# x kept in DRAM as two float16 halves scaled by batch, and an expert's rows turned by transposing DMAs instead of by TensorE

## The chip, the cores and the metric

One NeuronCore of a Trainium2 chip runs the whole program; the other seven are idle. The metric is the time of one execution in microseconds (us) as the device reports it. The engines are TensorE (PE, with its weight loads shown apart as PEld), VectorE (DVE), ScalarE (ACT), GpSimd (POOL) and SyncE (SP), which here only issues DMAs. Each engine works through its own instructions in the order in which they are written, and so does each queue of DMA issues.

## The reference, cut to what matters

```python
# attention: batch 4, heads 8, seq 768, head_dim 64, 16 clusters
q_assign = argmax(q_n @ c_n.T); k_assign = argmax(k_n @ c_n.T)
mask = q_assign[..., :, None] == k_assign[..., None, :]
attn = softmax(where(mask, scale * q @ k.T, -1e9)) @ v
x = attn.transpose(0, 2, 1, 3).reshape(3072, 512)
# mixture of experts: 8 experts, two for each row
noisy = x @ w_gate + log1p(exp(x @ w_noise)) * noise
top2 and their softmax weights wt, for each row
for e in range(8):
    out[rows of e] += wt * (relu(x[rows of e] @ w1[e]) @ w2[e])     # w1: 512x1024, w2: 1024x512
```

All inputs and the output are float32.

## The kernel before

**The attention** runs over 16 pairs of heads, four pairs to a batch. It is written as 192 steps, twelve for each pair. A step makes two score tiles of 128x384 (`scores`, L515), takes their exponential on ACT (L516), and four steps later multiplies an earlier step's exponentials by v (`values`, L544 to L550). Around this core a table `AT` and the function `at(step, f)` put every other piece of work at a third of a step: splitting q and k into halves (`a_split`, L382 to L392), the row maxima (`b_max`, L484 and L487), the cluster mask (`a_mask`, `b_mask`, L448 to L456), and loads. The order of each engine is this written order. All score tiles, transposes and small sums pass through one ring of six PSUM buffers (`ps()`, tile name `ring`): TensorE can't begin the seventh tile after one that ACT or VectorE has not yet read.

When the last pair of batch b is done, its x rows lie in `xt[b]` (128 partitions, six rows of 512 float32 each). `store_x(b)` writes them to the DRAM tensor `xs` in one DMA of 1.5 MB (L591), and `g_logits`, `g_logits2`, `g_turn`, `g_gate` and `g_list` work out the gate and write each row's number and weight into a table of the experts' rows. For batches 0 to 2 this lies among the steps of the next batch, from step 48b + 52 on. For batch 3 it lies in `experts`, beside the first expert's first layer.

**The experts** take at most 832 rows each, in seven tiles (six of 128, one of 64). For a tile, `gather_x` (POOL, L1125) fetches 128 rows of `xs` by an indirect DMA into `xg` (four buffers). `turn_x` (L1136) turns it: four transposes on TensorE into a ring buffer, and then `scaled_halves` writes a high and a low float16 half, times `sx`, into `xT` (ACT L1035, VectorE L1036). `sx` is one power of two for the whole of x: `x_max` takes the maximum of |v| over all batches (an upper bound of |x|), and `x_scale` (L1046 to L1057) makes `px` and its reciprocal `sx` from it. `layer1` (L1146) multiplies each of eight column blocks of w1 by `xT` in three products of halves, ACT and VectorE write relu halves into `hT`, and `layer2` (L1183; L1174 and L1177 for the short tile) makes 128 rows of output, which VectorE weighs (L1192) and POOL scatters (L1196).

There is one `xT`. The next expert's turns stand between this expert's second-layer tiles (`tail`), after its first layer has read `xT`. Weights go through seven staging buffers (`stg`, L1104 for w1, L1113 for w2), are reduced to a maximum and split into halves on ACT and VectorE.

The first expert is special: its first four tiles (`TA`) hold rows of batches 0 to 2 alone, so its first layer over these runs while batch 3 is gated; three further tiles are gathered after batch 3's list is known, and its first layer over them runs after the first four second-layer tiles.

## Time and profile before

| | us |
|---|---|
| median of 3 runs | 1087.87 (1086.75 to 1088.76) |
| the profiled execution | 1087.8 |
| its span, first to last instruction | 1086.0 |
| outside the span | 1.8 |
| TensorE busy | 1024.3 (94%) |
| VectorE busy | 702.7 (65%) |
| POOL busy | 550.4 (51%) |
| ACT busy | 533.7 (49%) |
| TensorE's granted clock, mean | 0.985 of full speed |

A busy time counts every instruction from start to end; matmuls overlap, so a busy TensorE is not one at its peak. "Idle before" is the time in which an engine had nothing running before an instruction, and the releaser is the event that ended it. Idle time counts only where it lies on the engine that sets the end.

### The profile page before, as it was taken

How to read it: one execution, taken by the hardware profiler on the slowest of the kernel's cores; microseconds unless marked ns; L12 is line 12 of the kernel's file. 1: busy time of each engine (PE TensorE's matmuls, PEld its weight loads, DVE VectorE, ACT ScalarE, POOL GpSimd, SP SyncE). 2: the span in 40 equal slices, each digit the busy share in tenths (PEclk: the TensorE clock that was granted, in tenths of full speed). 3: DMA queues.
4: the chain of work that ended last, by engine and by line, in shares of the span. 5: the costliest groups of instructions: out<-in, count | busy, mean ns of one | idle time of the engine just before them, and what ended most of it. 6: DMA issues, size and time to landing. Idle time of an engine off the chain costs nothing.

```text
span 1086.0 us, 22549 instructions
## 1 busy us (share of the span) xinstructions
PE 1024.3 (94%) x8733; PEld 705.0 (65%) x8733; DVE 702.7 (65%) x1484; ACT 533.7 (49%) x1090; POOL 550.4 (51%) x598
## 2 busy tenths in 40 slices
PE   5789999999999999979999999999999999999994
PEld 4678898889888988865555555555455555554542
DVE  5787776977688768998375656645655565556511
ACT  3467767766776766665144425334254152432510
POOL 9167675779677977831344233442352333513211
PEclk9799999999999999999999999999999999999997
DMA  7776767576757655252235235342352344422200
GB/s 199 170 186 145 177 157 201 143 170 156 206 141 177 155 158 116 81 176 93 98 114 174 92 110 174 117 136 100 125 183 72 100 160 137 136 82 77 59 33 34
DMA packets 87058, 144.48 MB, mean 133 GB/s; under 512 B 13689, under 2 KB 65273, under 8 KB 86434
## 3 DMA queue, kind: packets, MB, share of 16 engines
q1 hardware_dynamic: 73650, 106.61, 36.5%
q0 software_dynamic: 13296, 36.38, 10.3%
q8 instruction: 70, 1.15, 0.4%
q14 instruction: 42, 0.34, 0.1%
HBM read 78.21 MB, written 26.51 MB: 96 GB/s over the span
## 4 chain that ended last, share of the span: by engine, by line
PE 72%; DVE 10%; issue 8%; POOL 4%; DMA 3%; ACT 2%; SPq 0%; POOLq 0%; DVEq 0%; ACTq 0%
PE ring L1146 21%; PE ring L1183 20%; PE ring L515 9%; PE ring L484 5%; PE av L544 2%; PE ring L1136 2%; PE av L550 2%; PE av L546 2%; DMA A<-mk 2%; DVE aux L487 2%; PE ring L403 1%; DVE mm L487 1%; PE ring L382 1%; PE ring L418 1%; DVE pl L527 1%
## 5 line engine op out<-in xcount | busy, mean ns | idle before, releaser
L527 POOL TENSOR_TENSOR pl<-pe 128x768 f16<-128x768 f32 x173 | 251.7, 1469 | 80.7 <-ACT pe L516 78.7
L1146 PE MATMUL ring<-xT,w1t 128*128 128x416 f16 (+2 forms) x1536 | 274.9, 340 | 2.3 <-DVE xT L1036 2.3
L1183 PE MATMUL ring<-w2t,hT 128*128 128x512 f16 x1152 | 255.3, 379 | 0.0
L516 ACT ACTIVATE pe<-ring,l 128x384 f32<-128x384 f32 x384 | 201.6, 578 | 64.9 <-PE ring L515 59.9
L1146 PEld LDWEIGHTS <-w1t 128*128 128x128 f16 x1536 | 149.9, 98 | 121.6 <-issue 5.1
L1183 PEld LDWEIGHTS <-hT 128*128 128x128 f16 x1152 | 112.7, 98 | 127.1
L1196 POOL DMA_INDIRECT out<-yo,idx x52 | 62.8, 1208 | 210.1 <-DVE yo L1192 107.9
L487 DVE TENSOR_REDUCE aux<-ring 128x1 f32<-128x384 f32 x192 | 108.0, 562 | 73.0 <-PE ring L484 68.5
L1029 ACT ACTIVATE hr<-ring 128x416 f32<-128x416 f32 (+2 forms) x128 | 66.5, 520 | 161.7 <-PE ring L1146 161.4
L515 PE MATMUL ring<-A 128*128 128x384 f32 x384 | 141.5, 368 | 0.9 <-ACT pe L516 0.7
L1032 DVE TENSOR_TENSOR hT<-hr,hT 128x416 f16<-128x416 f32 (+3 forms) x128 | 71.5, 559 | 100.8 <-ACT hT L1031 100.7
L515 PE MATMUL ring<-B 128*128 128x384 f32 x384 | 129.9, 338 | 1.6 <-DMA B<-nt 1.6
L1125 POOL DMA_INDIRECT xg<-xs,idx x52 | 60.7, 1167 | 117.3 <-PE ring L1136 101.4
L484 PE MATMUL ring<-A 128*128 128x384 f32 x384 | 108.3, 357 | 12.0 <-DMA A<-mk 6.6
L1192 DVE SCALAR_TENSOR_TENSOR yo<-ring,we,xt 128x512 f32<-128x512 f32 (+1 forms) x49 | 36.7, 749 | 115.2 <-PE ring L1183 102.3
L487 DVE TENSOR_REDUCE mm<-ring 128x1 f32<-128x384 f32 x192 | 105.1, 548 | 0.0
L1035 ACT ACTIVATE xT<-ring,sx 128x512 f16<-128x512 f32 (+1 forms) x56 | 36.0, 659 | 139.2 <-PE ring L1136 139.2
L544 PE MATMUL av<-vv,pe 128*128 128x65 f16 x1152 | 97.1, 195 | 2.7 <-DVE xt L558 2.6
L546 PE MATMUL av<-vv,pe 128*128 128x64 f16 x1152 | 96.2, 192 | 0.0
L544 PEld LDWEIGHTS <-pe 128*128 128x128 bf16 x1152 | 79.5, 99 | 18.0 <-issue 11.5
L484 PEld LDWEIGHTS ring<-A 128*128 128x128 f32 x384 | 69.7, 191 | 23.5 <-ACT pe L516 9.6
L546 PEld LDWEIGHTS <-pe 128*128 128x128 bf16 x1152 | 77.8, 98 | 0.3
(208 smaller groups left out, 1530.5 us busy)
## 6 DMA issues: line engine op xcount, KB each, us to landing
stg<-in_moe_w SPq DMA_DIRECT2D x64, 512.0 KB
A<-hl SPq DMA_DIRECT2D x30, 384.0 KB
B<-hl SPq DMA_DIRECT2D x30, 384.0 KB
vt<-in_v SPq DMA_DIRECT2D x8, 768.0 KB
out<-zt SPq DMA_DIRECT2D x12, 512.0 KB
xs<-xt SPq DMA_DIRECT2D x4, 1536.0 KB
A<-hl SPq DMA_DIRECT2D x60, 96.0 KB
B<-hl SPq DMA_DIRECT2D x30, 192.0 KB
```

Of the source, the lines that this page charges most:

```text
L484: nc.tensor.matmul(t, A[:, 0, s, j * 128:j * 128 + 128], A[:, 1, s, n * 384:n * 384 + 384], start=True, stop=True)
L487: nc.vector.tensor_reduce(o, t, axis=X, op=OP.max, negate=True)
L515: nc.tensor.matmul(t, M[:, 1 - qi, s, ks], M[:, qi, s, ns], start=not qi, stop=bool(qi))
L516: nc.scalar.activation(pe[:, n], t, AF.Exp, bias=self.l64[:, 0:1], scale=self.scale)
L527: (nc.vector if last else nc.gpsimd).tensor_tensor(lo, pe, hi, op=OP.subtract)
L544: nc.tensor.matmul(av[:, j, :], ph[:, js], vv[:, hh, kj, 64:129], start=(kc == 0 and j == 0), stop=False, skip_group_check=True)
L546: nc.tensor.matmul(av[:, j, :64], ph[:, js], vv[:, hh, kj, 0:64], start=False, stop=False, skip_group_check=True)
L1029: nc.scalar.activation(r[:, :n], p, AF.Relu, scale=2.0 ** -HT)
L1032: nc.vector.tensor_tensor(h1, r[:, a:b], h0, op=OP.subtract)
L1146: nc.tensor.matmul(p, self.w1t[:, wi, c, f * 128:f * 128 + 128], self.xT[:, xi, c, n0:n1], start=(i == 0), stop=(i == 3 * ND - 1))
L1183: nc.tensor.matmul(p, self.hT[:, hi, f, t * 128:t * 128 + 128], self.w2t[:, wi, f], start=(i == 0), stop=(i == 3 * NF - 1))
L1196: i = nc.gpsimd.indirect_dma_start(out=self.out, out_offset=bass.IndirectOffsetOnAxis(ap=en[:r], axis=0), in_=yo[:r], in_offset=None, boun ...
```

## The change

x is scaled and split into float16 halves once, when a batch is stored, and `xs` holds both halves of a row side by side (1024 float16, the same 2 KB). `store_x` is cut into three pieces of two rows per partition: ACT makes the high half, VectorE the low one, SP stores the 512 KB piece. The piece's buffer `xh` is one tile of a pool in which a name has one buffer unless it asks for more: `pre` for batches 0 to 2, `mo` for batch 3. A gathered tile then needs nothing but turning, and `turn_x` becomes one `dma_start_transpose` on SP's queue, from `xg` (128 x 1024 float16) to all eight 128-column blocks of `xT`. The halves must be made before the last batch's maximum is known, so the scale is now taken for each batch alone (`px`, `sx` have four columns), and the gate's weight carries `px` of its batch. Places in the written order move: the pieces of a batch stand at steps z + 1.333, 2.667 and 4.0 (z = 48b + 52), batch 3's after `split_w2(0, i)`; the first four turns stand ahead of the list load; in `tail` three turns stand ahead of the first second-layer tile and one ahead of each further one.

```diff
-        self.px, self.sx = (consts.tile([128, 1], F32, name=n) for n in ("px", "sx"))
+        self.px, self.sx = (consts.tile([128, self.B], F32, name=n) for n in ("px", "sx"))
...
-                at(z + T["store"], self.store_x, b)
+                for c in range(3):
+                    at(z + 1.333 + 1.333 * c, self.store_x, b, c)
...
-            at(z - 45 + 2 * i, self.x_scale, i)
+            for b in range(B):
+                at((48 * b + 3 if b else 20) + 2 * i, self.x_scale, b, i)
             at(z - 6 + i, self.w1_scale, 0, i)
-        at(z - 46, self.x_max)
+        for b in range(B):
+            at(48 * b + 2 if b else 19, self.x_max, b)
...
-        self.xs = self.dram.tile([N, DM], F32, name="xs")
+        self.xs = self.dram.tile([N, 2 * DM], F16, name="xs")
...
-    def store_x(self, b):
-        W = self.NJ * self.DM
-        self.nc.sync.dma_start(rap(self.xs, b * 128 * W, [[W, 128], [1, W]]),
-                               self.xt[b].rearrange("p j c -> p (j c)"))
+    def store_x(self, b, c):
+        n = self.NJ // 3
+        W, V = 2 * self.NJ * self.DM, 2 * n * self.DM
+        pool = self.pre if b + 1 < self.B else self.mo
+        h = pool.tile([128, n, 2, self.DM], F16, name="xh")
+        x, s = self.xt[b][:, n * c:n * c + n], self.sx[:, b:b + 1]
+        self.nc.scalar.activation(h[:, :, 0], x, AF.Copy, scale=s)
+        self.nc.vector.scalar_tensor_tensor(h[:, :, 1], x, s, h[:, :, 0], op0=OP.mult, op1=OP.subtract)
+        self.nc.sync.dma_start(rap(self.xs, b * 128 * W + V * c, [[W, 128], [1, V]]), h.rearrange("p j i c -> p (j i c)"))
...
-        do(lambda: nc.scalar.activation(rf()[:, :, 0, 1], pm(1), AF.Copy))
+        do(lambda: nc.scalar.activation(rf()[:, :, 0, 1], pm(1), AF.Copy, scale=self.px[:, b:b + 1]))
...
-            v.tensor_tensor(rf()[:, :, 1, 1], pm(1), m(1), op=OP.mult)
+            v.scalar_tensor_tensor(rf()[:, :, 1, 1], pm(1), self.px[:, b:b + 1], m(1), op0=OP.mult, op1=OP.mult)
...
-        self.store_x(b)
+        late = AT["late"]
+        for t in range(TA):
+            self.turn_x(0, t)
         self.load_list(1)
-        late = AT["late"]
-        for t in range(TA - late):
-            self.turn_x(0, t)
...
-            if j == NJ - 1:
-                for t in range(TA - late, TA):
-                    self.turn_x(0, t)
...
             self.split_w2(0, i)
+            if i < 3:
+                self.store_x(b, i)
...
-                while done < T and done * (T - t0) < (t - t0 + 1) * T:
+                while done < T and done < (t + 3 if e else 4 * (t - t0 + 1)):
                     self.turn_x(n, done)
...
-            self.nc.vector.tensor_tensor(self.c1, self.pw1, self.px, op=OP.mult)
+            self.nc.vector.tensor_copy(self.c1, self.pw1)
...
-        xg = self.mw.tile([128, self.DM], F32, name="xg", bufs=4)
+        xg = self.mw.tile([128, 2 * self.DM], F16, name="xg", bufs=4)
...
-        p = self.ps().rearrange("p (c n) -> p c n", c=ND)
-        for c in range(ND):
-            nc.tensor.transpose(p[:, c, :r], xg[:r, c * 128:c * 128 + 128], self.ident[:r, :r])
-        self.scaled_halves(self.xT[:, :, :, t * 128:t * 128 + r], p[:, :, :r], self.sx)
+        nc.sync.dma_start_transpose(self.xT.rearrange("p i c n -> p (i c) n")[:, :, t * 128:t * 128 + r], xg[:r])
```

`x_max` and `x_scale` take the batch as an argument and work on its columns. The same edits stand in `extra`, the loop for an expert with more than 832 rows.

## Rows read from the trace of the kernel before

**Rows 1.** The page: busy us (share of the span) and instructions of each engine; the chain that ended last, by engine.
```profile
PE 1024.3 (94%) x8733; PEld 705.0 (65%) x8733; DVE 702.7 (65%) x1484; ACT 533.7 (49%) x1090; POOL 550.4 (51%) x598
PE 72%; DVE 10%; issue 8%; POOL 4%; DMA 3%; ACT 2%; SPq 0%; POOLq 0%; DVEq 0%; ACTq 0%
```
**Rows 2.** Busy time by stage: the stretch around batch 0's store, and one expert. After the stretch and its length come busy us (instructions) of PE, PEld, DVE, ACT and POOL, TensorE's granted clock, the DMA engines' busy share and GB/s.
```profile
160.00:190.00 30.00, 29.63 (x382) 25.41 (x380) 18.92 (x47) 21.51 (x48) 15.46 (x14) 1.00 0.75 202
...
716.80:788.50 71.70, 71.70 (x388) 37.60 (x387) 41.02 (x67) 27.22 (x55) 26.52 (x34) 1.00 0.38 121
```
**Rows 3.** TensorE in order of time through the tail of expert 1: its first turn and second-layer tile, its last turn and the short tile (start, us, instruction, count). Then all turns of the program by their line (duration ns min/median/max, first and last start).
```profile
607.00 0.60 PE L1136 MATMUL ring<-ident,xg 128*128 128x128 f32 x4
607.44 5.34 PE L1183 MATMUL ring<-w2t,hT 128*128 128x512 f16 x24
...
641.47 0.46 PE L1136 MATMUL ring<-ident,xg 64*128 64x64 f32 x4
641.86 1.90 PE L1174 MATMUL ring<-w2t,hE 128*128 128x512 f16 x8
...
L1136 PE MATMUL ring<-ident,xg x224: 221/273/330, 482.1 to 1000.5; 128*128 128x128 f32 x96, 64*128 64x64 f32 x16
```
**Rows 4.** TensorE through the tail of the first expert (expert 0), and its granted clock just after (length, PE busy, clock, DMA share, GB/s).
```profile
552.25 1.47 PE L1136 MATMUL ring<-ident,xg 128*128 128x128 f32 x12
553.56 5.34 PE L1183 MATMUL ring<-w2t,hT 128*128 128x512 f16 x24
558.74 1.04 PE L1136 MATMUL ring<-ident,xg 128*128 128x128 f32 x8
559.62 5.34 PE L1183 MATMUL ring<-w2t,hT 128*128 128x512 f16 x24
564.79 0.99 PE L1136 MATMUL ring<-ident,xg 128*128 128x128 f32 x8
565.72 1.90 PE L1174 MATMUL ring<-w2t,hE 128*128 128x512 f16 x8
...
571.57 5.53 PE L1146 MATMUL ring<-xT,w1t 128*128 128x416 f16 x21 [2.33 <-DVE xT L1036]
...
572.00:574.00 2.00, 2.00 (x8) 0.50 0.55 219
```
**Rows 5.** What a DMA takes from issue to use: the landing times of the 56 gathers of 256 KB; and a 4 KB load on SP, issued at 465.90, with the POOL instruction that waits for it.
```profile
DMA to landing us min/median/max: 3.2/4.0/5.8
...
465.90 0.33 SPq L792 DMA_DIRECT2D lst<-tbl  x1
...
468.44 1.47 POOL L1125 DMA_INDIRECT xg<-xs,lst  x1 [3.56 <-DMA lst<-tbl]
```
**Rows 6.** The DMA engines while batch 2's store of 1.5 MB moves with nothing ahead of it (stretch, length, granted clock, busy share, GB/s).
```profile
400.00:401.00 1.00, 1.00 0.93 393
```
**Rows 7.** SP's issues around batch 0's store (the second of two 768 KB loads for batch 1, then the store), and the DMA engines just then (columns as in rows 6).
```profile
167.12 1.20 SPq L324 DMA_DIRECT2D qk<-in_k  x1
...
172.82 0.53 SPq L591 DMA_DIRECT2D xs<-xt  x1
...
172.00:173.00 1.00, 1.00 1.04 384
174.00:175.00 1.00, 1.00 1.15 120
```
**Rows 8.** ACT (two lines), VectorE and TensorE (two lines) in order of time in the same stretch.
```profile
168.70 0.60 ACT L600 ACTIVATE gxT<-ring 128x512 f32<-128x512 f32 x1 [2.11 <-PE ring L598]
...
171.74 0.28 ACT L609 ACTIVATE lg<-ring 128x128 f32<-128x128 f32 x1
...
167.63 0.56 DVE L439 TENSOR_TENSOR oh<-ring,km 128x384 bf16<-128x384 f32 x1
...
171.25 0.42 PE L608 MATMUL ring<-gxT,wgn 128*32 128x128 f32 x8
...
173.16 0.49 PE L382 MATMUL ring<-ident,qk 128*128 128x128 f32 x3
```
**Rows 9.** ACT in batch 2's stretch, at the place that answers to 171.74 of rows 8.
```profile
395.23 0.28 ACT L609 ACTIVATE lg<-ring 128x128 f32<-128x128 f32 x1
```
**Rows 10.** The end of the first expert's first layer over its four early tiles: two splits of w2 on ACT, one on VectorE, and the start of the second layer.
```profile
507.26 1.15 ACT L1035 ACTIVATE w2t<-stg,sw 128x1024 f16<-128x1024 f32 x1
...
517.62 1.15 ACT L1035 ACTIVATE w2t<-stg,sw 128x1024 f16<-128x1024 f32 x1
...
508.79 1.27 DVE L1036 SCALAR_TENSOR_TENSOR w2t<-stg,sw,w2t 128x1024 f16<-128x1024 f32 x1
...
516.45 15.70 PE L1183 MATMUL ring<-w2t,hT 128*128 128x512 f16 x72
```
**Rows 11.** TensorE where the experts begin, and at the turns of the three late tiles.
```profile
482.14 1.50 PE L1136 MATMUL ring<-ident,xg 128*128 128x128 f32 x12
...
491.44 2.82 PE L1146 MATMUL ring<-xT,w1t 128*128 128x512 f16 x12
...
531.99 1.42 PE L1136 MATMUL ring<-ident,xg 128*128 128x128 f32 x12
533.34 5.35 PE L1183 MATMUL ring<-w2t,hT 128*128 128x512 f16 x24
```
**Rows 12.** The one TensorE transpose of a scale (here that of w1), with what it waited for.
```profile
468.27 0.27 PE L1046 MATMUL ring<-ident,wm 128*4 128x128 f32 x1 [0.81 <-DVE wm L1068]
```

More of the change, by code (lines that the diff above doesn't have):

```diff
@@ L988, in extra @@
                                       .rearrange("p e t c -> p (e t c)"))
-                    xg = self.mw.tile([128, DM], F32, name="xg", bufs=4)
+                    xg = self.mw.tile([128, 2 * DM], F16, name="xg", bufs=4)
                     nc.gpsimd.indirect_dma_start(out=xg, out_offset=None, in_=self.xs,
@@ L996, in extra @@
                                                  bounds_check=self.N - 1, oob_is_err=False)
-                    p = self.ps().rearrange("p (c n) -> p c n", c=ND)
-                    for c in range(ND):
-                        nc.tensor.transpose(p[:, c, :], xg[:, c * 128:c * 128 + 128], self.ident)
-                    self.scaled_halves(self.xT[:, :, :, 0:128], p, self.sx)
+                    nc.sync.dma_start_transpose(self.xT.rearrange("p i c n -> p (i c) n")[:, :, 0:128], xg)
                     for f in range(NF):
@@ L1036, in scaled_halves, with x_max @@
         self.nc.vector.scalar_tensor_tensor(dst[:, 1], st, s, dst[:, 0], op0=OP.mult, op1=OP.subtract)
-    def x_max(self):
+    def x_max(self, b):
         self.xm = self.wk.tile([128, 1], F32, name="xm", bufs=1)
-        self.nc.vector.reduce_max(self.xm, self.vm.rearrange("p g h -> p (g h)"), axis=X)
+        self.nc.vector.reduce_max(self.xm, self.vm[:, 2 * b:2 * b + 2].rearrange("p g h -> p (g h)"), axis=X)
     def scale_a(self, m):
@@ L1057, in scale_b, with x_scale @@
         nc.vector.reciprocal(s, p)
-    def x_scale(self, i):
+    def x_scale(self, b, i):
         if i == 0:
@@ L1062, in x_scale @@
         else:
-            self.scale_b(self.xg_, self.fx, self.px, self.sx)
+            self.scale_b(self.xg_, self.fx, self.px[:, b:b + 1], self.sx[:, b:b + 1])
     def max_w1(self, e, c):
@@ L1133, in turn_x @@
         xg = self.xg.pop((e, t))
-        p = self.ps().rearrange("p (c n) -> p c n", c=ND)
-        for c in range(ND):
-            nc.tensor.transpose(p[:, c, :r], xg[:r, c * 128:c * 128 + 128], self.ident[:r, :r])
-        self.scaled_halves(self.xT[:, :, :, t * 128:t * 128 + r], p[:, :, :r], self.sx)
+        nc.sync.dma_start_transpose(self.xT.rearrange("p i c n -> p (i c) n")[:, :, t * 128:t * 128 + r], xg[:r])
     def layer1(self, e, f, parts):
```

## The prediction

> **What bounds the kernel now.** I read the page first, then the busy times by stage, then TensorE in order of time. The page gives TensorE 94% of the span, and the chain that ended last runs 72% through it [rows 1]. By stage it is closer still: around batch 0's store TensorE is busy 29.63 of 30.00 us, and through a whole expert 71.7 of 71.7, at full clock [rows 2]. So an instruction taken from TensorE is time saved, if nothing else is late, and a wait that reaches TensorE is time lost. The other engines show how much room the moved work has: beside an expert ACT is busy 27.22 of 71.7 us, but around batch 0's store 21.51 of 30 [rows 2]. The change moves work from the first place to the second.
>
> The sum is made against the profiled execution, 1087.8 us (span 1086.0 and 1.8 around it), 0.07 below the median.
>
> **What it removes.** 56 turns of four transposes (224 matmuls) [rows 3], each with a pass on ACT and one on VectorE that nothing waits for in the tails.
>
> *Tails of experts 1 to 6.* From the start of a turn to the second-layer tile behind it are 0.44 us, for the short tile 0.39 [rows 3]; 6 x 0.44 + 0.39 = 3.0 us a tail, six tails: **18.2 us**. This is the firm term. Its cover: the turns must be done before the next first layer. A tail's second layer lasts 34.2 us without them (607.00 to the short tile's end near 644, less 3.0). Three turns wait for nothing but the end of the first layer, a fourth has its rows too, and three wait for gathers. The weight loads behind them on SP, which ran ahead in before, then start in the tail; each is needed a tile or more after its place, so I cost them at nothing, and 1 us a tail if that is wrong.
>
> What a transposing DMA takes no row shows. From below: 256 KB at 393 GB/s [rows 6] is 0.7 us and a small load is used 2.5 us after its issue [rows 5], so 3.2 in all, 0.7 to 1.3 apart. From above: 5.8 us, the slowest landing of the same 256 KB by a gather [rows 5], one at a time. I take the lower, as these bytes stay in SBUF and a gather's are 128 separate rows. Then four turns and the three gathers behind them end some 13 us into a tail, with 21 to spare.
>
> The Trainium skill has two rules here, and they disagree. "VectorE: DVE Perf Modes", under The three transpose paths, gives 1309 ns for a 128x128 block by DMA against 390 on TensorE and advises TensorE where PSUM will do. That would make a turn of eight blocks 10.5 us (an estimate from that page), seven of them 73, and speaks against the change. "Advanced Engine Details and Errata", under X-Bar Transpose (TRN2), has such DMAs as fast as plain ones, which is the lower end above. No row of before decides.
>
> *Tail of expert 0.* Its turns take 1.31 + 0.88 + 0.93 = 3.1 us of TensorE; then the first layer stands 2.33 us waiting for xT, after which the granted clock is 0.50 (1.2 GHz instead of 2.4), and 21 matmuls take 5.53 us [rows 4] instead of 3.7 (192 take 33.9 in the next experts' layers): 1.8 more. Together 7.2. Here the cover is short: the second layer lasts 13.2 us, and the turns' chain is 3.2 to the first landing, 1.3 x 2 for the POOL issues of the later two gathers, 1.0 + 4.0 for the last of these [rows 5], and 3.2 for its turn: 14. I leave 1.5 us of wait, and save **5.7**.
>
> *Opening and late tiles.* The first layer starts at 491.44, 9.3 us after the turns begin at 482.14 [rows 11]. Without them the gate's front moves up by some 2.6 us, but four DMAs from 482.3, 1.3 apart, land at 489.8: 1.6 saved. The late tiles' turns (1.35) [rows 11] go: **3.0** in all. Savings: 26.9.
>
> **What it adds.** Twelve pieces of 1.15 us on ACT and 1.27 on VectorE, by the same form in the splits of w2 [rows 10]. Not their length matters, but `xh`: it is one buffer, so ACT can't begin a piece until the DMA of the piece before has landed, and behind ACT wait the exponentials. A piece's cycle is 1.15 + 1.27 + landing, and landing is 2.5 + 1.3 (0.5 MB at 393 GB/s) = 3.8: 6.3 us [rows 5, 6]. The places are 4 to 5 us apart.
>
> *Batches 0 and 1.* The first piece fits in ACT's idle 2.11 us before 168.70, and VectorE takes it once free at 168.2 [rows 8]; SP can issue at 169.5. But 1.5 MB of q and k was issued up to 168.3, and the queue moves in order: 384 GB/s until a dip to 120 at 174 to 175, where small mask transfers follow, and only then batch 0's store [rows 7]. So the piece's bytes come at 174.0 to 175.4, and I take it as landed at 176.0 (ends: 175.4 and 176.6). ACT comes to the second piece at 171.7, before `lg` [rows 8], and stands until 176.0; `lg` is read at 177.5. TensorE goes on until the seventh ring tile after that of 171.25: tiles of L608, L598, twice L515, twice L484, then L382 at 173.16 [rows 8]. It stands from 173.2 to 177.5, **4.3 us**. The third piece: the second's store lands at 177.2 + 1.3 + 3.8 = 182.3; ACT has by then worked through 3.3 us of backlog, reaches it at 180.5, and is 3.0 late after it, half of which the ring covers: **1.5**. Two batches: 11.6. Two idle stretches of 4.3 us, longer than the 2.33 after which the clock fell [rows 4], cost 1.5 each in matmuls at half clock: 3.0.
>
> *Batch 2.* Nothing is ahead of the first piece: landed at 396.5, ACT due at 395.2 [rows 9]. By the same count 1.4 and 1.5: **2.9**.
>
> *Smaller.* VectorE's 1.27 in front of row maxima: 0.3 a batch, 0.9. Three more scales: their transpose takes 0.27 and waited 0.81 once [rows 12]; between 0.2 and 1.1 each I take 0.4, as they have a step of their own to wait: 1.2. Behind the waiting store on SP stand a maximum's row and the next pair's halves, both due steps later: nothing. Attention: **19.6**.
>
> *Batch 3.* Its pieces stand between the splits of w2, ACT and VectorE in turn. By cycles of 6.3 from 509 the third piece is on ACT at 521 to 522, the last relu and the last split of w2 behind it, and VectorE ends that split at 526. The second layer starts at 516.45 [rows 10] and needs it after six of its eight blocks, at 520.4: **5.6** of wait, and 1.5 of clock. The late gathers then land by 535, before 543 when their tiles are used. Added in all: 26.7.
>
> Sum: 1087.8 - 26.9 + 26.7 = **1087.6**; as the bounds of the landing and of the clock lean to less (no fall of the clock in a wait that ends sooner), I round down to **1087**: no change that shows. (About 0.2%, 2.2 us, is what a measurement of this kernel can tell from none.)
>
> **Rivals.**
>
> *The waits are mostly covered.* If a piece lands 1 us sooner than I take it, the third pieces and all of batch 2 fall inside what the ring covers, the clock stays up, and batch 3's wait halves: added are two waits of 3.3, 2.1 of smaller ones and 2.8, 11.5, and the time is 1072. For it: the ring covered every wait on ACT in before [rows 2]. Against: q and k are in the queue ahead, whatever a landing takes.
>
> *Each held piece costs its whole cycle (slower).* The place is ACT at the second and third piece of each batch, eight times. If landing takes 2 us longer (a store to DRAM confirmed later than a load, SP held behind another wait), each costs 2 more: 16, and 1103. It decides from 0.4 us a piece, 3 us in all. For it: the DMA engines are 75% busy there and over 100% from 172 on [rows 2, 7]. Against: the 2.5 us of the small load.
>
> *The transposes are slow, or don't run as block moves at all.* At 5.8 us one by one a tail lasts 40.6 instead of 34.2: 6.4 x 6 = 38; expert 0's tail 40.6 instead of 14.7: 26; the opening's four 23 instead of 7.5: 16; 1167. It shows from 4.9 us a turn (34.2 / 7). By the skill's 10.5 us a turn, in "VectorE: DVE Perf Modes", it would be far more. For it: nothing in the rows. Against: SP has little else to do.
>
> **How the numbers follow.** Forecast 0.50, own range 1079 to 1095; covered waits 0.21; whole cycles 0.20; slow transposes 0.09. Of the forecast's half, 0.21 lies below 1085.7, 0.18 within 0.2%, 0.11 above. Faster: 0.21 + 0.21 = 0.42; same 0.18; slower 0.11 + 0.20 + 0.09 = 0.40. The range 1072 to 1103 leaves out the slow transposes, a good third of the covered waits and the far end of the whole cycles.
>
> **What would show it.** Right: the tails' second-layer tiles 5.18 us apart with no turn between, a period near 68.7 instead of 71.7; TensorE idle 4 to 5 us at L382 in batches 0 and 1, released by ACT, and ACT's own wait at the second piece put down to the DMA of `xs`; an idle of 5 to 6 us in the first tile of layer 2. Wrong: waits on `xT` put down to the transposing DMA in tails of experts 1 to 6; no wait on ACT at the pieces; or the experts' period unchanged.

## The result and the profile after

The changed kernel takes 1095.99 us (median of 4 runs, 1094.86 to 1097.35), beside 1087.59 for the kernel before on the same chip: a ratio of 1.0077, 95% interval 1.0060 to 1.0094. The forecast was 1087, no change that shows; the changed kernel is slower by 0.8%, and the interval lies above 1. The profiled execution took 1094.86 us, with a span of 1092.6, which is 6.6 more than before.

Its page: busy time by engine, the chain that ended last by engine, and the DMA packets (answering [rows 1]).

```profile
PE 1013.3 (93%) x8518; PEld 685.8 (63%) x8518; DVE 687.4 (63%) x1455; ACT 512.0 (47%) x1046; POOL 549.1 (50%) x598
PE 63%; DVE 13%; issue 8%; DMA 7%; POOL 4%; SPq 2%; ACT 2%; POOLq 0%; DVEq 0%; ACTq 0%
DMA packets 143247, 158.08 MB, mean 145 GB/s; under 512 B 68857, under 2 KB 120441, under 8 KB 143138
```

TensorE is busy 11.0 us less than before and the program is 6.6 longer, so TensorE stands or waits 17.6 us more. In the chain TensorE's share falls from 72% to 63%, and DMA's rises from 3% to 7%. By stage (columns as in [rows 2]; one whole expert after, then 30 us of batch 0's stretch from 169.19, before and after):

```profile
735.98:804.57 68.59, 68.59 (x359) 34.59 (x360) 36.54 (x60) 22.84 (x48) 25.00 (x34) 1.00 0.55 153
...
169.19:199.19 30.00, 29.85 (x378) 25.79 (x377) 19.73 (x55) 24.34 (x55) 18.64 (x16) 1.00 0.74 199
...
169.19:199.19 30.00, 26.01 (x301) 20.79 (x297) 16.33 (x37) 20.14 (x43) 12.37 (x9) 0.89 0.49 146
```

An expert is 68.59 long where it was 71.70, with TensorE busy throughout: this gain is there in full. Around batch 0's store TensorE is busy 26.01 of 30 where it was 29.85, and its mean clock is 0.89. So the loss is in attention.

How the 6.6 comes about, by the starts of the same instruction before and after (last column: the prediction's terms). A mask pass is ACT's pass that writes the cluster mask `mk`, four to a batch; a relu is ACT's pass on `hr`:

```
stretch                                              before   after    change   forecast
start to the 6th mask pass of ACT                    143.29   143.80   + 0.5      0
6th to 16th mask pass (the three batches' pieces)    281.66   304.76   +23.1    +19.6
16th mask pass to the first relu of the experts       69.35    70.12   + 0.8    - 1.6
first relu to expert 0's last (batch 3's pieces)      58.15    62.69   + 4.5    + 5.8
expert 0's last relu to expert 1's first (its tail)   24.57    21.14   - 3.4    - 5.7
expert 1's first relu to the last pass on yo         494.50   475.55   -18.9    -18.2
```

(The fourth forecast is 5.6 + 1.5 less the 1.35 of the late tiles' turns.) The loss is in attention, and ACT shows where: its nine passes on `xh` in batches 0 to 2 (start, us, then in brackets how long it stood before, and for what).

```profile
167.49 1.15 ACT L598 ACTIVATE xh<-xt,sx 128x1024 f16<-128x1024 f32 x1
177.26 1.15 ACT L598 ACTIVATE xh<-xt,sx 128x1024 f16<-128x1024 f32 x1 [4.46 <-DMA xs<-xh]
183.17 1.15 ACT L598 ACTIVATE xh<-xt,sx 128x1024 f16<-128x1024 f32 x1 [0.33 <-DMA xs<-xh]
...
286.91 1.15 ACT L598 ACTIVATE xh<-xt,sx 128x1024 f16<-128x1024 f32 x1
296.84 1.15 ACT L598 ACTIVATE xh<-xt,sx 128x1024 f16<-128x1024 f32 x1 [4.62 <-DMA xs<-xh]
302.44 1.15 ACT L598 ACTIVATE xh<-xt,sx 128x1024 f16<-128x1024 f32 x1 [1.51 <-DMA xs<-xh]
...
407.00 1.15 ACT L598 ACTIVATE xh<-xt,sx 128x1024 f16<-128x1024 f32 x1
415.11 1.15 ACT L598 ACTIVATE xh<-xt,sx 128x1024 f16<-128x1024 f32 x1 [2.80 <-DMA xs<-xh]
420.32 1.15 ACT L598 ACTIVATE xh<-xt,sx 128x1024 f16<-128x1024 f32 x1 [1.11 <-DMA xs<-xh]
```

The six waits sum to 14.8 us. The forecast had 14.5 for TensorE in the same places (4.3 + 1.5 twice, and 2.9). By batch they are 4.8, 6.1 and 3.9 against 5.8, 5.8 and 2.9, so that the sum agrees so closely is in part luck. TensorE then stands where the forecast said, at L382 of before (L385 now) behind ACT's `lg`, in batches 0 and 1:

```profile
178.63 0.90 PE L385 MATMUL ring<-ident,qk 128*128 128x128 f32 x3 [3.65 <-ACT lg L617]
...
298.20 0.55 PE L385 MATMUL ring<-ident,qk 128*128 128x128 f32 x3 [2.57 <-ACT lg L617]
```

After 3.65 us of standing the granted clock is 0.50 (1.2 GHz of 2.4) from 178 to 184, after 2.57 it stays at 1.00 (stretch, length, busy time of PE, PEld, DVE, ACT, POOL, clock, DMA share, GB/s):

```profile
178.00:180.00 2.00, 1.37 (x16) 1.30 (x17) 1.55 (x2) 2.00 (x6) 0.00 (x0) 0.50 0.04 8
...
299.00:303.00 4.00, 3.38 (x42) 2.42 (x38) 1.70 (x4) 2.29 (x6) 1.47 (x1) 1.00 0.35 135
```

So the waits are right in place and nearly right in size, and yet attention loses 23.1, not 14.8. And VectorE's pass, 1.27 us elsewhere, is three times as long in batch 2's first piece (and 3.32 in batch 1's). VectorE and POOL in order of time:

```profile
408.41 3.87 DVE L599 SCALAR_TENSOR_TENSOR xh<-xt,sx,xh 128x1024 f16<-128x1024 f32 x1
...
402.51 7.17 POOL L530 TENSOR_TENSOR pl<-pe 128x768 f16<-128x768 f32 x5
409.62 0.15 POOL L361 MEMSET vv<- 128x48 f16 x1
409.72 1.47 POOL L530 TENSOR_TENSOR pl<-pe 128x768 f16<-128x768 f32 x1
```

VectorE's pass is issued into a run of POOL's subtracts and ends 1.1 us after the run's last one (412.28 against 411.19).

**Theory** for the experiments: the gain in the tails is as forecast, and attention spends it by ACT's waits for the single buffer `xh`. **Rival**: the 29 us of work that the pieces add to ACT and VectorE cost the time, whatever the buffer. A third possibility is that the transposing DMAs, with 56189 more packets, cost something of their own.

### The profile page after: what moved, and what is told of

Read it like the earlier page. It is cut to its first block, busy times and chain, and to the rows that moved or that the text cites. A ratio compares the mean times of both kernels' runs of the same rounds, so it can differ in the third digit from the quotient of the medians.

```text
span 1092.6 us, 22148 instructions
## 1 busy us (share of the span) xinstructions
PE 1013.3 (93%) x8518; PEld 685.8 (63%) x8518; DVE 687.4 (63%) x1455; ACT 512.0 (47%) x1046; POOL 549.1 (50%) x598
## 4 chain that ended last, share of the span: by engine, by line
PE 63%; DVE 13%; issue 8%; DMA 7%; POOL 4%; SPq 2%; ACT 2%; POOLq 0%; DVEq 0%; ACTq 0%
PE ring L1146 19%; PE ring L1183 17%; PE ring L518 8%; PE ring L487 4%; DMA A<-mk 2%; DVE aux L490 2%; PE av L547 2%; PE av L553 2%; PE av L549 2%; DVE mm L490 2%; DMA xs<-xh 1%; PE ring L406 1%; PE ring L385 1%; DVE pl L530 1%; DVE xh L599 1%
## 5 line engine op out<-in xcount | busy, mean ns | idle before, releaser
L1128 POOL DMA_INDIRECT xg<-xs,idx x52 | 54.6, 1050 | 145.0 <-DMA xT<-xg 120.4
L487 PEld LDWEIGHTS ring<-A 128*128 128x128 f32 x384 | 69.4, 190 | 30.5 <-ACT pe L519 13.6
L518 PEld LDWEIGHTS ring<-A 128*128 128x128 f32 x384 | 73.3, 191 | 2.7 <-ACT pe L519 1.2
```

What stands on the lines that cost most here:

```text
L487: nc.tensor.matmul(t, A[:, 0, s, j * 128:j * 128 + 128], A[:, 1, s, n * 384:n * 384 + 384], start=True, stop=True)
L518: nc.tensor.matmul(t, M[:, 1 - qi, s, ks], M[:, qi, s, ns], start=not qi, stop=bool(qi))
```

## Experiments

Ratios are to the kernel before on the same chip, with 95% intervals; multiplied by 1087.6 they compare with the expectations. Attention is always the stretch from ACT's 6th mask pass to its 16th.

**Gain and work apart.** Four kernels on one chip.

`e1_turns`: no pieces, the stores read a constant.

```diff
-        self.nc.scalar.activation(h[:, :, 0], x, AF.Copy, scale=s)
-        self.nc.vector.scalar_tensor_tensor(h[:, :, 1], x, s, h[:, :, 0], op0=OP.mult, op1=OP.subtract)
-        self.nc.sync.dma_start(rap(self.xs, ..., [[W, 128], [1, V]]), h.rearrange("p j i c -> p (j i c)"))
+        self.nc.sync.dma_start(rap(self.xs, ..., [[W, 128], [256, V // 256], [1, 256]]),
+                               self.xq[:, None, :].to_broadcast([128, V // 256, 256]))
```

> Left out: the pieces on ACT and VectorE. The stores have the same places and bytes, but read one constant buffer that holds a part of x as halves, so the experts work on other rows. The transposing DMAs stay. Theory (holds: the change loses by what waits for the single buffer xh, and gains in the tails as forecast): the gain alone is seen, 18.7 us in the tails of experts 1 to 6 and 3.4 in expert 0's, less about 1 for the scales by batch: 1066 (1062 to 1070). Rival (the transposing DMAs cost something elsewhere, by their many small packets beside the weight loads): above 1072.

Measured 0.9802 (0.9778 to 0.9826), 1066.1: the gain alone, as expected. The many small packets cost nothing that shows, so the third possibility falls. Expert 0's tail is 19.36 here, 5.2 less than before, where the forecast had 5.7.

`e2_nohold`: as `e1_turns`, with both passes of every piece kept.

> Left out: the halves are computed as in the changed kernel, all twelve pieces on ACT and VectorE at their places, but the stores read the constant buffer of e1_turns, so no piece waits for a store. Theory (holds): within 8 us of e1_turns, 1066 to 1074, and no wait of ACT at the pieces. Rival (the 29 us of added ACT and VectorE work in attention cost the time themselves, with VectorE slowed beside POOL): 1085 or more, near the changed kernel's 1096.

Measured 0.9884 (0.9859 to 0.9909), 1075.0, 8.9 above `e1_turns`. The waits for stores are gone, and most of the loss with them; but it is 1 us above the theory's range (1066 to 1074): the work itself costs nearly 9 us. TensorE over attention, `e1_turns` and then `e2_nohold` (columns as above):

```profile
143.31:425.80 282.49, 273.34 (x3552) 247.68 (x3552) 217.32 (x570) 196.46 (x411) 216.75 (x196) 1.00 0.67 165
```
```profile
143.62:434.68 291.06, 276.95 (x3552) 247.26 (x3552) 231.75 (x579) 205.72 (x420) 217.82 (x196) 1.00 0.65 160
```

The same 3552 matmuls at the same clock; TensorE's idle time goes from 9.2 to 14.1, and its passes are 3.6 longer. ACT is busy 205.72 of 291.06, 71%: a mean with room in it, and the work is paid all the same.

`e3_six`: six half pieces and two buffers in the same space.

```diff
-        n = self.NJ // 3
+        n = self.NJ // 6
...
-        h = pool.tile([128, n, 2, self.DM], F16, name="xh")
+        h = pool.tile([128, n, 2, self.DM], F16, name="xh", bufs=2)
...
-                for c in range(3):
-                    at(z + 1.333 + 1.333 * c, self.store_x, b, c)
+                for c in range(6):
+                    at(z + 1.333 + 0.667 * c, self.store_x, b, c)
```

> The same sums in six pieces of half the size a batch and two buffers, in the same SBUF space and the same stretch of steps. Theory (holds): two pieces are in flight, a cycle of 0.6 + 0.65 + 2.7 us for every two pieces, so six take 11.9 us where their places span 8.8; a batch loses some 3 us where it lost 6 to 7: 1078 to 1086. Rival (work): unchanged, 1094 to 1098, or worse by the fixed cost of twelve more instructions on either engine.

Measured 0.9975 (0.9957 to 0.9993), 1084.9, within the theory's range. ACT's waits in attention fall from 14.8 to 8.7, and attention by 6.5.

`e4_pieces`: TensorE turns the stored halves.

```diff
-        nc.sync.dma_start_transpose(self.xT..., xg[:r])
+        p = self.psum.tile([128, 2, ND, 128], F16, name="ring", bufs=6)
+        for c in range(2 * ND):
+            nc.tensor.transpose(p[:, c // ND, c % ND, :r], xg[:r, c * 128:c * 128 + 128], self.idh[:r, :r])
+        nc.scalar.activation(self.xT[:, 0, :, t * 128:t * 128 + r], p[:, 0, :, :r], AF.Copy)
+        nc.vector.tensor_copy(self.xT[:, 1, :, t * 128:t * 128 + r], p[:, 1, :, :r])
```

> Undone: the transposing DMAs. TensorE turns the stored halves (eight 128x128 float16 transposes a turn), ACT and VectorE copy them to xT; the pieces stay. Theory (holds): the loss alone is seen: 1096 + 18.7 + 3.4 = 1118 (1113 to 1122). Rival (the transposing DMAs cost something elsewhere): below 1112.

Measured 1.0205 (1.0178 to 1.0231), 1109.9: below the theory's range, and what I had named for the rival. The profile tells why, in part: from expert 1's first relu to the end are 494.3 us, 18.8 more than in the changed kernel, as expected; but expert 0's tail is 20.40 with TensorE's turns in it, 0.7 less than with the DMAs, where I had added 3.4. So the sum was too simple. The two profiled executions are 18.8 us apart and the ratios only 13.9; that difference stays open, but no stretch of the trace shows a hidden cost of the DMAs.

**More buffers.** `e5_six3` is `e3_six` with a third buffer; tables of the start move to space that is used later.

```diff
-        h = pool.tile([128, n, 2, self.DM], F16, name="xh", bufs=2)
+        h = pool.tile([128, n, 2, self.DM], F16, name="xh", bufs=3)
...
-        jp = consts.tile([128, 128], F32, name="jp")
+        s0 = self.gp.tile([128, 4, 128], F32, name="gxT", bufs=2)
+        jp = s0[:, 0]
```

> As e3_six, with three buffers of half a piece (tables that are read only at the start give up their space). Theory (holds): three stores in flight, (0.72 + 0.73 + 2.7) / 3 = 1.4 us a piece, which is less than the 1.5 us between places; what is left is the first landing of batch 0 behind q and k. Attention's loss falls from e3_six's 17.0 us to about the 9.8 of e2_nohold, the work alone: 1085 - 7 = 1078 (1075 to 1081). Rival (the price is the added instructions, which are as many as in e3_six): 1083 or more.

Measured 0.9898 (0.9876 to 0.9921), 1076.5. One number differs from `e3_six` in the pieces, the count of buffers, and the time falls by 8.4. ACT's first wait in batch 0, with two buffers and then with three:

```profile
176.59 0.72 ACT L598 ACTIVATE xh<-xt,sx 128x512 f16<-128x512 f32 x1 [3.25 <-DMA xs<-xh]
```
```profile
177.06 0.72 ACT L600 ACTIVATE xh<-xt,sx 128x512 f16<-128x512 f32 x1 [0.80 <-DMA xs<-xh]
```

This version computes what the other two do and is faster than both.

`e6_open` adds TensorE's turns (as in `e4_pieces`) for expert 0's first four tiles alone, and a buffer for each piece of batch 3.

```diff
+        if e == 0 and t < self.TA:
+            p = self.psum.tile([128, 2, ND, 128], F16, name="ring", bufs=6)
...
+            return
         nc.sync.dma_start_transpose(self.xT..., xg[:r])
```

> As e5_six3, and expert 0's first four turns by TensorE from the stored halves again (eight float16 transposes each), where the trace shows TensorE idle for 4 us before the last rows of attention; in batch 3 every piece has its own buffer. Theory: the transposing DMAs at the opening cost about 2 us there by the gap and the clock behind it, and batch 3's holds 1 to 2: 2 to 4 us below e5_six3, 1074 to 1076. Rival (TensorE's 2.6 us for the four turns are paid as before): within 1 us of e5_six3.

Measured 0.9893 (0.9864 to 0.9921): no difference, as the rival had it. From the 16th mask pass to the first relu are 70.55 us, 71.11 in `e5_six3`, 70.12 in the changed kernel, 69.35 before: what the opening lost is not got back by TensorE's turns.

`e7_hiV` gives the high halves of batches 0 to 2 to VectorE.

```diff
-        self.nc.scalar.activation(h[:, :, 0], x, AF.Copy, scale=s)
+        (self.nc.vector.tensor_scalar(h[:, :, 0], x, s, None, op0=OP.mult) if b + 1 < self.B else
+         self.nc.scalar.activation(h[:, :, 0], x, AF.Copy, scale=s))
```

> As e6_open, with the high half by VectorE too in batches 0 to 2, so that ACT has no part in a piece there. If what the work costs is ACT's share of it (the exponentials behind): 3 to 6 us below e6_open, 1069 to 1072. If it is VectorE's (its pass waits beside POOL's run of subtracts, and the row maxima behind it): the same or 1 to 4 us above e6_open.

Measured 0.9930 (0.9907 to 0.9953), 1080.0, 4.0 above `e6_open`: work on VectorE is dearer there than on ACT. Its high half has one tensor as input and takes 0.47 us alone; issued into POOL's run it stands too, 2.82 us in batch 1 and this in batch 2:

```profile
401.42 2.87 DVE L602 TENSOR_SCALAR xh<-xt,sx 128x512 f16<-128x512 f32 x1
```

`e8_later` moves the six places by two thirds of a step.

```diff
-                    at(z + 1.333 + 0.667 * c, self.store_x, b, c)
+                    at(z + 2 + 0.667 * c, self.store_x, b, c)
```

> As e6_open, each piece two thirds of a step (about 1.5 us) later, so that in batches 1 and 2 the first pass of VectorE comes after POOL's run of subtracts or near its end. If a pass waits for POOL while POOL has a run of subtracts: the first low halves of batches 1 and 2 take 0.75 to 1.9 us instead of 3.1 and 3.3, and the time is 1 to 3 us below e6_open. If the long passes have another cause that belongs to the first piece: still 3 us, and the time unchanged.

Measured 0.9910 (0.9888 to 0.9933): half of what I expected came. The first low halves of batches 1 and 2 take 0.88 and 1.06 us instead of 2.78 and 3.10, so it is POOL's run that holds them; but the time is the same. The third and the sixth low half of each batch now take 1.51 (0.74 alone), and over the three batches the low halves stand nearly as long as in `e6_open`: by their lengths above 0.74, 5.9 us against 6.6. So this run doesn't tell what the standing costs.

**The changed kernel with one thing different.** `e9_shift`: only the places, two thirds of a step later.

```diff
-                    at(z + 1.333 + 1.333 * c, self.store_x, b, c)
+                    at(z + 2 + 1.333 * c, self.store_x, b, c)
```

> The changed kernel (three pieces, one buffer) with each piece two thirds of a step later, nothing else. Theory: in batches 1 and 2 the first low half no longer waits beside POOL's run of subtracts (1.3 to 1.6 us instead of 3.3 and 3.9), and as the single buffer makes each piece wait for the whole chain before it, the second piece's hold there falls by about 2 us: attention's loss 23.7 - 4 = 20, the time 1091 to 1094. Rival (the hold is the store's landing alone, whatever VectorE does): within 1.5 us of 1096.

Measured 0.9969 (0.9948 to 0.9989), 1084.2: 12 us off the changed kernel by a shift of two thirds of a step, more than twice what I expected. The passes of VectorE are as foretold (1.28 us for the 3.32 and 3.87), but batch 0, which had no such pass, gains as well:

```profile
170.38 1.14 ACT L598 ACTIVATE xh<-xt,sx 128x1024 f16<-128x1024 f32 x1
177.22 1.15 ACT L598 ACTIVATE xh<-xt,sx 128x1024 f16<-128x1024 f32 x1 [1.79 <-DMA xs<-xh]
```

The first store is issued 2.7 us later (172.86 for 170.19) and lands at the same time, 177.2. ACT has simply done other work meanwhile: its wait is 1.79 where it was 4.46, and the third piece's is gone. In the three batches ACT now waits 5.5 us, and attention is 9.6 shorter. None of VectorE's nine passes stands any more (1.28 or 1.29 us each).

`e10_twice`: each turn of experts 1 to 7 issued twice.

```diff
-        nc.sync.dma_start_transpose(self.xT..., xg[:r])
+        for _ in range(1 if e == 0 else 2):
+            nc.sync.dma_start_transpose(self.xT..., xg[:r])
```

> The changed kernel with every turn by DMA made twice for experts 1 to 7 (the second writes the same again). By the forecast four turns and the gathers behind them end some 13 us into a tail of 31 us, so the doubled ones of experts 2 to 7 are still hidden: the experts' period stays at 68.6. Only expert 0's tail, of 10 us, loses 3 to 6: 1099 to 1102. Rival (the turns are near what the tail hides): the period grows by 1 us or more, 1105 or above.

Measured 1.1070 (1.1039 to 1.1101), 1204: by its size the rival's (1105 or above), but not for the rival's reason. I had overlooked that the second writes what the first has written, so SP waits for the first to land, with the weight loads behind it. In the tail of expert 1 (SP in order of time; TensorE's wait at its end):

```profile
655.66 1.33 SPq L1138 DMA_TRANSPOSE xT<-xg  x1
658.83 1.23 SPq L1138 DMA_TRANSPOSE xT<-xg  x1
...
675.58 1.24 SPq L1138 DMA_TRANSPOSE xT<-xg  x1
681.62 1.23 SPq L1138 DMA_TRANSPOSE xT<-xg  x1
...
696.18 0.38 PE L1049 MATMUL ring<-ident,wm 128*4 128x128 f32 x1 [13.13 <-DVE wm L1085]
```

As a trial of the cover it fails; as a measurement it is good. A turn takes 3.2 us from issue until SP may go on with nothing beside it (655.66 to 658.83), and 6.0 behind a weight load (675.58 to 681.62); over all tails a turn behind a weight load took 4.4 to 7.7. The forecast's ends were 3.2 and 5.8. And it shows what holds the gain up: that no turn has to wait for the one before on SP.

`e11_poolq`: the stores of batches 0 to 2 on POOL's queue.

```diff
-        self.nc.sync.dma_start(rap(self.xs, ...
+        (self.nc.gpsimd if b + 1 < self.B else self.nc.sync).dma_start(rap(self.xs, ...
```

> The changed kernel with the stores of batches 0 to 2 issued by POOL, whose queue holds no loads of q and k. Forecast's step (a piece's bytes wait in SP's queue behind q and k): in batch 0 the first landing falls from 7.1 us to 3 to 4 and the second piece's wait of 4.5 us nearly goes; batch 1's likewise by 2; batch 2 unchanged: 1088 to 1092. Rival (the 16 DMA engines are shared, so the order of a queue matters little): landing 5 us or more in batch 0 and the time within 2 us of 1096.

Measured 1.0053 (1.0035 to 1.0072), 1093.4, between the two ranges; but attention is 304.7 us and ACT's waits 14.9, as in the changed kernel (304.8 and 14.8). Batch 0's first store goes out at 172.96 and ACT goes on at 180.97, 8.0 us later (batch 2, quiet: 4.1, against 2.8 from SP's queue). A queue with nothing ahead doesn't help. That the bytes of q and k share the 16 DMA engines fits this: they moved 359 GB/s from 172 to 176 (347 in the changed kernel).

`e12_wider`: `e5_six3` with its places over 4.0 steps, and a buffer for each piece of batch 3.

```diff
-                    at(z + 1.333 + 0.667 * c, self.store_x, b, c)
+                    at(z + 1.333 + 0.8 * c, self.store_x, b, c)
```

> e5_six3 with the six places of a batch spread over 4.0 steps instead of 3.3, and a buffer for each piece in batch 3. If what is left is ACT and VectorE being late for TensorE where pieces stand close: 1 to 3 us below e5_six3's 0.9898 of before (1074 to 1076). If it is the work itself: within 1 us of it.

Measured 0.9900 (0.9873 to 0.9926): the same. What is left is not got by wider places.

**Whose work?** Both kernels are `e2_nohold` with one of the two passes left out.

`e13_actonly`:

```diff
-        self.nc.vector.scalar_tensor_tensor(h[:, :, 1], x, s, h[:, :, 0], op0=OP.mult, op1=OP.subtract)
```

> As e2_nohold, with VectorE's low halves left out. If ACT's added 9 x 1.15 us in attention are what is paid (the exponentials behind them late for TensorE): attention 5 us or more longer than e1_turns, the time 1071 or above. If VectorE's are: within 3 us of e1_turns, 1066 to 1069. I expect the two shares about equal: 1069 to 1072.

`e14_vonly` (`lo` has the same size; `xc` is the constant, broadcast):

```diff
-        self.nc.scalar.activation(h[:, :, 0], x, AF.Copy, scale=s)
-        self.nc.vector.scalar_tensor_tensor(h[:, :, 1], x, s, h[:, :, 0], op0=OP.mult, op1=OP.subtract)
+        self.nc.vector.scalar_tensor_tensor(lo, x, s, xc, op0=OP.mult, op1=OP.subtract)
```

> As e2_nohold, with ACT's high halves left out (VectorE subtracts the constant buffer instead). If VectorE's added 9 x 1.28 us and its passes beside POOL are what is paid (row maxima late): attention 5 us or more longer than e1_turns, 1071 or above. If ACT's are: 1066 to 1069. With about equal shares: 1069 to 1072, and the two shares add up to e2_nohold's 9.

Measured 0.9834 (0.9796 to 0.9872), 1069.5, and 0.9854 (0.9823 to 0.9884), 1071.7. The intervals overlap. By these times the shares are 3.4 and 5.6 us, together about the 8.9 of `e2_nohold`. Attention is 282.5 in `e1_turns`, 283.9 with ACT's passes, 287.1 with VectorE's, 291.1 with both: 1.4 and 4.6, with 2.6 left over. Single profiles differ too much (by up to 3.5 us, see below) to settle the split or to say what the 2.6 are; both counts, and `e7_hiV`, put VectorE's share above ACT's. In `e14_vonly` the passes beside POOL's run are long again (here batch 1), without a piece of ACT before them:

```profile
281.73 3.72 DVE L604 SCALAR_TENSOR_TENSOR xh<-xt,sx,xq 128x1024 f16<-128x1024 f32 x1
287.49 1.28 DVE L604 SCALAR_TENSOR_TENSOR xh<-xt,sx,xq 128x1024 f16<-128x1024 f32 x1
```

**All runs together.** What attention lost against before, ACT's waits for stores in the three batches, and the loss less these waits:

```
kernel        attention  lost   ACT's waits  rest
before          281.7
changed         304.8    23.1      14.8       8.3
e4_pieces       306.5    24.8      15.2       9.6
e11_poolq       304.7    23.0      14.9       8.1
e10_twice       301.3    19.6      16.1       3.5
e3_six          298.3    16.6       8.7       7.9
e9_shift        295.2    13.5       5.5       8.0
e5_six3         290.7     9.0       1.4       7.6
e12_wider       290.6     9.0       1.0       8.0
e6_open         290.5     8.8       0.9       7.9
e8_later        291.1     9.4       0.9       8.5
e7_hiV          296.1    14.4       0        14.4
e2_nohold       291.1     9.4       0         9.4
e14_vonly       287.1     5.5       0         5.5
e13_actonly     283.9     2.2       0         2.2
e1_turns        282.5     0.8       0         0.8
```

Each us that ACT waits is about a us of attention, and some 8 us stay in the kernels that split each piece between ACT and VectorE; with the whole piece on VectorE (`e7_hiV`) it is 14.4. One row stands out, `e10_twice`, whose attention has the same code as the changed kernel's: single profiles differ by up to 3.5 us here, and a difference in this table below that is not settled.

## Why the prediction was wrong

It forecast 26.9 saved and 26.7 added, and 1087, no change that shows; the program became 0.8% slower. The time is 1 us above the likeliest case's own range (1079 to 1095), on the side that had 0.40 of the chance.

*What held.* The tails of experts 1 to 6: 18.9 us against 18.2, the period 68.59 against "near 68.7", and no wait on `xT` in them: in expert 1's tail the last of seven turns is issued 15.1 us after the first (647.63 and 632.50), with 34 us of second layer to hide in. The late tiles: 1.35 less in `e1_turns` from the first relu to expert 0's last (56.80 for 58.15), against 1.35. The scales by batch: 0.8 of attention in `e1_turns`, against 1.2. ACT's waits at the pieces: 14.8 against 14.5, in the places named.

*The turn by DMA.* Taken as 3.2 us, measured in `e10_twice` as 3.0 to 3.2 with no load beside it (the first of each tail from expert 1 on, and 655.66), and 4.4 to 7.7 behind a load. The rival of slow transposes put its mark at 4.9 us a turn done one by one; turns behind loads passed it there, yet no tail of the changed kernel from expert 1 on waits for them, as a turn needn't wait for the one before. The Trainium skill's "VectorE: DVE Perf Modes" (The three transpose paths) would make it 10.5 for eight blocks, by the prediction's estimate from that page; this trace doesn't agree. It is nearer the Trainium skill's "Advanced Engine Details and Errata" (X-Bar Transpose (TRN2)), that such DMAs are as fast as plain ones: a gather of the same bytes landed after 3.2 to 5.8 us [rows 5].

*The step that failed first:* "Not their length matters, but `xh`". The prediction put the pieces themselves into idle time (ACT's 2.11 us before 168.70, VectorE "once free") and left 0.9 + 1.2 us beside the waits, with 3.0 more for the clock. The runs showed some 8 us that no buffer takes away (8.9 by the times of `e2_nohold` and `e1_turns`, with attention's clock at 1.00 in both), more of it by VectorE's passes than by ACT's: 5.6 and 3.4 by the times, whose intervals overlap. Which instructions are late by it was not found. The busy shares of that stretch, 21.51 and 18.92 of 30 [rows 2], had told me there was room.

*That VectorE would stand beside POOL was there to be foreseen.* The low half has two inputs in SBUF, and POOL's subtracts run back to back in batches 1 and 2. Three low halves that I followed (batches 1 and 2 of the changed kernel, batch 1 of `e14_vonly`) ended 1.1 us after POOL's last subtract: 291.92 against 290.83, 412.28 against 411.19, 285.45 against 284.36. The Trainium skill has the rule, in "SBUF — State Buffer" (SBUF: two separate sides): VectorE with two SBUF inputs and a GpSimd instruction that reads SBUF share one pair of ports as an exclusive lock for a whole instruction. The trace agrees, and adds that POOL's next subtract went ahead of the waiting VectorE each time: it began at 289.37, 409.72 and 282.90, when the low half had been issued at 288.60, 408.41 and 281.73. Batch 2, costed at 2.9 ("Nothing is ahead of the first piece"), is one place: its low half is 2.6 us late, ACT waits 3.9, and the segment of attention around it loses 7.9 us, as much as those of batches 0 and 1 (8.0 each). But as far as single profiles tell, the standing is not the 8 us: in `e9_shift` no pass stands and the rest is 8.0, in the changed kernel two stand, 4.6 us in all, and it is 8.3. That the standing costs by way of the single buffer, as part of ACT's waits, is argued; no run has it apart.

*The clock.* Forecast 3.0 us in batches 0 and 1, by the 2.33 us of [rows 4]. It fell in batch 0 after 3.65 us of standing and not in batch 1 after 2.57. No run isolates its price in attention. Since the rest is no larger in the changed kernel (8.3) than in `e2_nohold` (9.4), where the clock stays at 1.00, it adds little that shows to the waits; but TensorE is busy 281.24 us over attention there and 276.95 in `e2_nohold`, so it may be part of what the waits cost.

*Expert 0's tail:* 5.7 forecast, 3.4 measured. The wait was sized well (1.5 forecast, 2.0 measured). But it is the clock behind it that decides, and the forecast had taken its 1.8 us as saved: in the changed kernel it falls, in `e5_six3`, with a wait of 1.9, it doesn't. The changed kernel, then `e5_six3`, in the 4 us in which the wait ends:

```profile
596.00:600.00 4.00, 3.30 (x11) 1.54 (x12) 2.60 (x4) 0.00 (x0) 1.01 (x2) 0.64 0.78 283
```
```profile
578.00:582.00 4.00, 2.59 (x15) 1.49 (x16) 3.45 (x4) 0.00 (x0) 0.23 (x1) 1.00 0.68 235
```

The tail is 21.1 in the one and 19.3 in the other: 3.4 and 5.3 saved. The length of the wait doesn't tell them apart: in `e6_open`, with 1.9 as well, the clock falls and the tail is 21.0.

*The opening:* 1.6 saved by forecast, 0.8 lost. The prediction moved the gate's front up by 2.6 us, the length of TensorE's turns. (By its own terms four DMAs from 482.3 land at 489.4, not 489.8; that is 0.4 us.) But the turns had stood where TensorE has nothing else to do: the front waits for the last rows of attention, `xt`, which VectorE writes. So the time from TensorE's last products with `pl`, POOL's subtracts (481.95 before, 506.14 after) to the first layer (491.44 and 515.89) is 9.49 us before and 9.75 after, no shorter; the other half us of the loss lies ahead of these products, where the kernels range from 57.0 to 58.9 us. TensorE is idle now in that wait, and the clock behind is lower:

```profile
508.09 1.13 PE L606 MATMUL ring<-ident,xt 128*128 128x128 f32 x5 [1.23 <-DVE xt L561]
...
504.00:508.00 4.00, 1.44 (x27) 1.08 (x27) 3.93 (x8) 0.00 (x0) 0.00 (x0) 1.00 0.02 4
508.00:512.00 4.00, 3.91 (x29) 2.44 (x29) 4.00 (x6) 2.31 (x5) 0.00 (x0) 0.57 0.78 150
```

The lower clock is not what the opening lost. `e6_open` filled the gap with TensorE's turns, the clock stayed at 1.00, and the same stretch took 9.69:

```profile
496.00:500.00 4.00, 2.98 (x42) 2.18 (x40) 3.77 (x9) 3.60 (x8) 0.00 (x0) 1.00 0.00 0
```

*Batch 3:* 7.1 forecast (5.6 of wait and 1.5 of clock), 5.9 measured (the 4.5 of the stretch and the 1.4 that the late tiles' turns no longer take). The place is right, the wait is too dear: TensorE waited 1.2 + 0.9 us in the second layer's first tile, not 5 to 6.

```profile
546.90 0.38 PE L1183 MATMUL ring<-w2t,hT 128*128 128x512 f16 x1 [1.21 <-ACT w2t L1038]
548.22 18.47 PE L1183 MATMUL ring<-w2t,hT 128*128 128x512 f16 x77 [0.94 <-DVE w2t L1039]
```

The pieces came every 5.9 and 5.2 us on ACT, not every 6.3. These 77 matmuls took 1.7 us more than at the rate of before (72 in 15.70 [rows 10]), near the forecast's 1.5 of clock. The rest lies in two waits for VectorE that the forecast did not have, 0.6 at 537.62 and 1.0 at 579.25. So the total came out nearly right in part by luck.

Of the 6.7 us between the forecast's terms and the change of the span, attention makes 3.5, the opening 2.4, expert 0's tail 2.3, the start 0.5, and batch 3 and the tails give back 2.0.

*The rivals.* "Each held piece costs its whole cycle" named the right place and sign, at eight pieces. Its price, a landing 2 us longer, was not the cause: the quiet landing was 2.7 to 3.4 us (issue to ACT's next piece in batch 2 and at the third pieces of 0 and 1), below the 3.8 taken; only the first stores of batches 0 and 1 took longer, 7.1 and 4.9. "Mostly covered" asked for 1072; even with nothing held the work keeps it at 1075.

What stays open: which of TensorE's passes get longer by the added work (of 8.6 us between `e1_turns` and `e2_nohold`, 5.0 are idle time and 3.6 are not), and why its granted clock falls behind a wait in some kernels and not in others.

## What to carry to other kernels

Work moved to engines that are 60 to 75% busy is not free because the mean has room: cost it by what is late in that very stretch (here some 8 us), and look for passes that stand beside POOL's, which can cost where something waits for them. A buffer that waits for its own store holds ACT, and attention with it, about a us for a us; three buffers of half the size gave back all that the change had lost and more (1.0077 to 0.9898), places where ACT has other work until the landing gave 12 of these 19 us (0.9969). A turn by DMA that hides behind 34 us of matmuls is a clear gain, as long as nothing makes the queue wait for each one.

## What was not expected of the hardware

- A pass of VectorE with two SBUF inputs (1.28 us alone) took 3.3 to 3.9 us when issued into a back-to-back run of POOL's subtracts, and ended 1.1 us after the run. So did one with a single tensor as input in `e7_hiV`: 2.8 to 2.9 us for 0.47, ending 0.3 us after the run.
- A store of 512 KB to DRAM behind 1.5 MB of loads let ACT go on after 7.1 us from SP's queue and 8.0 from POOL's, with 2.8 and 4.1 in quiet.
- TensorE waited 1.9 to 2.1 us at the same instruction in several kernels; the granted clock in the 4 us around the end of the wait was 1.00 in some and 0.57 to 0.71 in others, worth 1.8 us.
- A turn of 256 KB by DMA took 3.0 to 3.2 us alone and 4.4 to 7.7 behind a 512 KB load, and some 1000 packets.
